# Another order of the SBUF pools in a fused attention and MLP kernel

## The chip, the cores and the metric

The kernel runs on one core of a Trainium2 chip. The metric is the device time of one execution in microseconds (us); the median of three runs of the kernel before is 382.42 us (380.60 to 382.48).

## What is computed

Three layers follow each other. The first is attention with a decaying state, over 2 batches, 8 heads, 768 positions and 64 elements per head. The second and third are gated feed-forward layers with a model width of 512 and an inner width of 1024. All data are float32.

```python
for t in range(S):                                    # attention, per head
    state = gamma * state + k[t] (outer) v[t]
    y[t] = scale * q[t] @ state
xk = mu_k * x + (1 - mu_k) * x_prev                   # second layer; x is y, heads joined
xr = mu_r * x + (1 - mu_r) * x_prev
v = relu(xk @ w_k) ** 2 @ w_v
x = sigmoid(xr @ w_r) * v
h = gelu(x @ w_in); u, v = halves of h                # third layer
v_n = (v - mean) / sqrt(var + 1e-6) * g_ln
out = x + (u * (w_sg @ v_n + b_sg)) @ w_out           # w_sg mixes the 768 positions
```

## The kernel before

The whole kernel is one straight list of operations. A planner (`Plan`) simulates the five engines with costs per operation and puts them in an order; each engine then runs its operations in exactly that order. The planner knows the tile pools by name, with a number of buffers for each.

The attention stage takes 12 chunks of 128 positions. For each, PE computes scores (sc, L407), the state (st, L443) and the output (y, L461 for the part from the state, L469 for the part within the chunk). These matmuls are plain float32, and a trace shows two PE instructions for each. sc uses two halves of 64 partitions side by side; the y matmul of L461 uses all 128 partitions.

Everything after it works on blocks of 512 columns (2 batches by 256 positions, 3 blocks). Each operand is split into a high part in fp32r and the rest, also in fp32r, and a product is made of three passes (high by high, high by low, low by high). `dense` (L310) issues all of these matmuls, so that they all have line L318. The groups are, in the trace's names: kp<-xo,wk (moving operand xo, stationary wk), rp<-xo,wr, vp<-k,wv, vp<-win,x2o (moving win, stationary x2o), up<-x2o,win, sp<-wsg,vh (moving wsg, 256 columns, the rest have 512) and op<-gt,wout. In the trace's names the moving operand doesn't always stand first; in the code it is `rhs`.

ACT and DVE convert the weights from the 8-byte words in which they are loaded (raw), into a tile cv and from there into the two fp32r tiles (hi by a cast at L237, lo by a subtraction at L289). They also clear out the PSUM results. After a kp tile ACT applies relu (L523), two squares (L528, L530), and DVE subtracts (L531). SP issues all DMAs.

Where each pool lies in SBUF follows from the order in which the pools are entered, one after the other from byte 16512 of each partition. The order is that of the dictionary `slots` (L196), and `cp`, with the constants, is the last.

```python
for name in slots:
    space = dict(space=bass.MemoryType.PSUM) if name == "ps" else {}
    pools[name] = ctx.enter_context(tc.tile_pool(name=f"{name}_p", bufs=slots[name], **space))
```

| pool | bytes per partition | start before | start mod 64 | what is in it |
|---|---|---|---|---|
| p4 | 17 x 4096 | 16512 | 0 | chunk, pr, xo, k (k2), x2o, vh, bsg |
| x | 3 x 8224 | 86144 | 0, 32, 0 | x and x2 |
| t | 8 x 2048 | 110816 | 32 | vs, cv, mix, rk, u, g, o |
| raw | 3 x 4096 | 127200 | 32 | weights as loaded, v of the third layer |
| small | 384 | 139488 | various | bn statistics and norm |
| aA, aB | 2 x 8192 each | 139872, 156256 | 32 | wk, then win, then gt |
| bA, bB | 2 x 9216 each | 172640, 191072 | 32 | scr (attention), wv, wsg |
| cA | 2 x 8192 | 209504 | 32 | wr, then wout |

The x pool's buffers are 8224 bytes, which is 32 more than a multiple of 64; three of them move what comes behind by 32. The PSUM pool ps has its own memory. Within a pool the buffers of p4, t, raw and of the weights are multiples of 64 bytes long, and the matmuls' columns in them begin at multiples of 512 bytes.

Of the kernel before, what the change touches and what calls it, by code (L numbers as in the profile page):

```python
# [28 lines left out]
NB = S // BW  # L29
# [163 lines left out]
def fused_kernel(ctx, tc, qk, kv, w_k, w_v, w_r, w_in, w_sg, w_out, consts, ydec, b_sg, out):  # L193
    nc = tc.nc
    pe, act, dve, pool, sp = nc.tensor, nc.scalar, nc.vector, nc.gpsimd, nc.sync
    slots = {"p4": 17, "x": NB, "t": 8, "raw": 3, "ps": 8, "small": 2, "aA": 1, "aB": 1, "bA": 1, "bB": 1, "cA": 1}  # L196
    plan = Plan(slots, {"p4": {"chunk": 6, "pr": 2, "xo": 4, "k2_0": 2, "k2": 8}, "ps": {"sc": 4, "y": 1},
                        "t": {"vs": 2, "cv": 2, "mix": 2, "rk": 2, "u": 6, "g": 2, "o": 2}},
                {("p4", "chunk"): 6, ("p4", "xo"): 8, ("t", "cv"): 4, ("ps", "sc"): 4})
# [584 lines left out]
```

## Time and profile before

| | us |
|---|---|
| median of 3 runs | 382.42 (380.60 to 382.48) |
| the profiled execution, its own time | 383.29 |
| its span, first to last instruction | 381.5 |
| PE busy | 370.1 |
| DVE busy | 248.6 |
| ACT busy | 159.0 |

Roughly, the attention stage runs until 54.8 us, the second layer until 226.5 us, the third layer's first product until 293.7 us, then sp and op in turn to 377.7 us. How to read it: the span holds one execution. PE is the matmul engine, DVE and ACT the two elementwise engines, POOL a third, and SP issues the DMAs. A busy PE is not PE at its peak, because matmuls are pipelined: the "mean ns of one" of a matmul covers its whole passage, and the distance from one start to the next is the shorter number that sets the time. The chain of work that ended last gives that distance, as the time of a piece divided by its count.

### The profile page before, as it was taken

The numbers are of one execution on the slowest core, as the hardware profiler recorded it, in microseconds if no ns is written. First come the engines' busy times: TensorE is split into PE (matmuls) and PEld (weight loads), VectorE is DVE, ScalarE is ACT, GpSimd is POOL, SyncE is SP. The second block draws the span as 40 slices with busy tenths as digits, with TensorE's granted clock in tenths as the row PEclk, the third lists the DMA queues.
The fourth block names the chain that finished last, engine by engine and source line by source line (L and its number), as shares of the span: only waits on it lengthen the run. The fifth ranks groups of instructions, "written<-read, shape, count | busy, mean of one in ns | idle before, by whom it ended". The sixth has DMA issues, their size and how long they took to land.

```text
span 381.5 us, 5546 instructions
## 1 busy us (share of the span) xinstructions
PE 370.1 (97%) x2218; PEld 308.8 (81%) x2218; DVE 248.6 (65%) x468; ACT 159.0 (42%) x266; POOL 20.1 (5%) x27
## 2 busy tenths in 40 slices
PE   6979999989999999999999999999999999999996
PEld 3978878868888888888888888888888999899884
DVE  2799999898898377312898637849385555516522
ACT  1357368998865575004889214414243000000000
POOL 2334510000000000000000000000000000000000
PEclk9889999989999999999999999999999999999999
DMA  7999455245530003300043101110111000020022
GB/s 263 415 363 411 190 168 165 70 145 159 180 111 0 0 3 110 110 2 0 9 158 110 42 2 41 27 54 3 41 44 41 2 0 2 27 84 0 29 110 82
DMA packets 11112, 35.97 MB, mean 94 GB/s; under 512 B 1232, under 2 KB 1360, under 8 KB 11088
## 3 DMA queue, kind: packets, MB, share of 16 engines
q1 hardware_dynamic: 11088, 35.63, 27.5%
q8 instruction: 17, 0.28, 0.3%
q14 instruction: 7, 0.06, 0.0%
HBM read 32.48 MB, written 3.15 MB: 93 GB/s over the span
## 4 chain that ended last, share of the span: by engine, by line
PE 90%; DMA 6%; DVE 1%; SPq 1%; ACT 1%; POOLq 0%; issue 0%
PE vp L318 26%; PE kp L318 18%; PE sp L318 13%; PE rp L318 9%; PE up L318 9%; PE op L318 9%; DMA chunk<-qk 3%; DMA scr<-ydec 2%; PE sc L407 2%; PE y L469 2%; DMA chunk<-kv 1%; PE y L461 1%; PE st L443 1%; DVE cv L285 0%; DVE cv L278 0%; DVE pr L416 0%
## 5 line engine op out<-in xcount | busy, mean ns | idle before, releaser
L318 PE MATMUL kp<-xo,wk 128*128 128x512 f32 x288 | 67.8, 395 | 0.0
L318 PE MATMUL vp<-k,wv 128*128 128x512 f32 x288 | 67.7, 395 | 0.0
L318 PEld LDWEIGHTS vp<-k,wv 128*128 128x128 f32 x288 | 54.0, 187 | 13.2
L318 PEld LDWEIGHTS kp<-xo,wk 128*128 128x128 f32 x288 | 53.9, 187 | 13.3 <-issue 0.2
L318 PEld LDWEIGHTS sp<-wsg,vh 128*128 128x128 f32 x432 | 51.4, 188 | 0.2
L318 PE MATMUL sp<-wsg,vh 128*128 128x256 f32 x432 | 51.4, 281 | 0.0
L318 PE MATMUL rp<-xo,wr 128*128 128x512 f32 x144 | 35.9, 409 | 1.8 <-ACT xo L237 1.8
L318 PEld LDWEIGHTS rp<-xo,wr 128*128 128x128 f32 x144 | 28.1, 195 | 9.2 <-ACT xo L237 2.3
L318 PE MATMUL vp<-win,x2o 128*128 128x512 f32 x144 | 34.1, 396 | 0.0
L318 PE MATMUL up<-x2o,win 128*128 128x512 f32 x144 | 34.1, 395 | 0.0
L318 PE MATMUL op<-gt,wout 128*128 128x512 f32 x144 | 33.1, 390 | 0.0
L318 PEld LDWEIGHTS vp<-win,x2o 128*128 128x128 f32 x144 | 27.1, 188 | 6.6
L318 PEld LDWEIGHTS up<-x2o,win 128*128 128x128 f32 x144 | 27.0, 187 | 6.6
L318 PEld LDWEIGHTS op<-gt,wout 128*128 128x128 f32 x144 | 26.9, 188 | 5.5
L531 DVE TENSOR_TENSOR k<-rk,k 128x512 fp32r<-128x512 f32 x24 | 16.6, 691 | 16.7 <-ACT rk L530 16.5
L528 ACT ACTIVATE k<-rk 128x512 fp32r<-128x512 f32 x24 | 15.2, 632 | 28.4 <-DVE rk L525 28.0
L543 DVE TENSOR_TENSOR x<-vp,x 128x512 f32<-128x512 f32 x12 | 8.3, 691 | 27.5 <-PE vp L318 27.5
L673 DVE SCALAR_TENSOR_TENSOR g<-sp,con,bsg 128x512 f32<-128x512 f32 x12 | 9.0, 752 | 26.0 <-PE sp L318 26.0
L285 DVE SCALAR_TENSOR_TENSOR cv<-raw,cv 128x512 int32<-128x512 int32 x32 | 24.5, 766 | 0.9
L263 ACT ACTIVATE cv<-raw 128x512 f32<-128x512 f32 x32 | 21.0, 667 | 3.3 <-DMA raw<-w_k 2.6
L689 DVE TENSOR_TENSOR o<-op,x 128x512 f32<-128x512 f32 x12 | 8.3, 692 | 20.4 <-PE op L318 20.3
L407 PE MATMUL sc<-chunk 64*128 64x128 f32 x192 | 15.7, 309 | 4.2 <-DMA chunk<-qk 4.2
(78 smaller groups left out, 425.2 us busy)
## 6 DMA issues: line engine op xcount, KB each, us to landing
chunk<-qk SPq DMA_DIRECT2D x12, 512.0 KB, 8.9
chunk<-kv SPq DMA_DIRECT2D x12, 512.0 KB, 8.5
raw<-w_k SPq DMA_DIRECT2D x8, 512.0 KB, 6.0
raw<-w_v SPq DMA_DIRECT2D x8, 512.0 KB, 3.7
raw<-w_in SPq DMA_DIRECT2D x8, 512.0 KB, 3.6
out<-o SPq DMA_DIRECT2D x12, 256.0 KB, 2.0
raw<-w_sg SPq DMA_DIRECT2D x6, 384.0 KB, 3.3
raw<-w_r SPq DMA_DIRECT2D x4, 512.0 KB, 4.5
```

Source lines behind the costliest of these rows:

```text
L263: plan.op("ACT", .68, lambda: act.activation(out=xf(), in_=word(1).bitcast(F32), func=ACTF.Copy, scale=F64_REBIAS), r=[(raw, 0)], w=[(xb, ...
L285: plan.op("DVE", .69, lambda: dve.scalar_tensor_tensor(out=xi(), in0=word(1), scalar=F64_SIGN, in1=xi(), op0=ALU.bitwise_and, op1=ALU.bitw ...
L318: pe.matmul(out=T[ps][:, cols], lhsT=l(), rhs=r(), start=first and q == 0 and i == 0, stop=q == 2 and i == len(grp) - 1, skip_group_check= ...
L407: pe.matmul(out=T["sc", i, p][:, j * CH:(j + 1) * CH], lhsT=a[par[p], 1, j], rhs=a[par[p], 0, j], start=j == 0, stop=j == KD - 1, skip_gro ...
L443: pe.matmul(out=st[par[p], b, j], lhsT=T["kv", i][:, 0, h], rhs=T["vs", i][:, h], start=c == 0 and b == 0 and j == 0, stop=b == B - 1 and ...
L461: pe.matmul(out=T[y][:, j * CH:(j + 1) * CH], lhsT=T["sbd", (c - 1) % 2][:, b, j], rhs=T["qk", i][:, 0, j], start=j == 0, stop=False, skip ...
L469: pe.matmul(out=T[y][par[p], j * CH:(j + 1) * CH], lhsT=T["vs", i][:, 2 * j + p], rhs=T["pr", i][:, p, j], start=c == 0 and j == 0, stop=j ...
L528: plan.op("ACT", .63, lambda: act.activation(out=T[o][:, 0], in_=T[rk], func=ACTF.Square), r=[(rk, 0)], w=[(o, ("hi", 0))], new=[new_p("k2 ...
L531: plan.op("DVE", .69, lambda: dve.tensor_tensor(out=T[o][:, 1], in0=T[rk], in1=T[o][:, 0], op=ALU.subtract), r=[(rk, 0), (o, ("hi", 0))], ...
L543: plan.op("DVE", .69, lambda: dve.tensor_tensor(out=T[x2][:, m], in0=T[ps], in1=T[x2][:, m], op=ALU.mult), r=[(ps, 0)], w=[(x2, m)])
L673: plan.op("DVE", .75, lambda: dve.scalar_tensor_tensor(out=seg(T[g]), in0=seg(T[ps]), scalar=T["vec"][:, 2, m:m + 1], in1=T["bsg"][:, cols ...
L689: plan.op("DVE", .69, lambda ps=ps, o=o, m=m: dve.tensor_tensor(out=T[o], in0=T[ps], in1=T["x2", n][:, m], op=ALU.add), r=[(ps, 0), (("x2" ...
```

## The change

The dictionary `slots` has the same entries with the same numbers, in another order: first the weight pools, then p4, raw, t, (ps,) and last x and small.

```diff
-    slots = {"p4": 17, "x": NB, "t": 8, "raw": 3, "ps": 8, "small": 2, "aA": 1, "aB": 1, "bA": 1, "bB": 1, "cA": 1}
+    slots = {"aA": 1, "aB": 1, "bA": 1, "bB": 1, "cA": 1, "p4": 17, "raw": 3, "t": 8, "ps": 8, "x": NB, "small": 2}
```

By the sizes above the pools then start at 16512 (aA), 32896 (aB), 49280 (bA), 67712 (bB), 86144 (cA), 102528 (p4), 172160 (raw), 184448 (t), all 0 mod 64; the three x buffers at 200832, 209056 and 217280, which are 0, 32 and 0 mod 64; small at 225504, and cp at 225888 as before.

## Rows read from the trace of the kernel before

**Rows 1.** The page: span, and busy time (share) and instructions by engine.
```profile
span 381.5 us, 5546 instructions
PE 370.1 (97%) x2218; PEld 308.8 (81%) x2218; DVE 248.6 (65%) x468; ACT 159.0 (42%) x266; POOL 20.1 (5%) x27
```

**Rows 2.** Waits of PE: who waited for whom: total us, times, longest.
```profile
PE sc L407 <- DMA chunk<-qk: 4.2, 2, 2.3
...
PE rp L318 <- ACT xo L237: 1.8, 1, 1.8
...
PE y L469 <- POOL vs L421: 0.4, 1, 0.4
```

**Rows 3.** The chain that ended last, in time: start us, us, what, count.
```profile
79.96 12.31 PE rp L318 x45
92.27 22.40 PE vp L318 x96
114.67 22.40 PE kp L318 x96
137.07 11.20 PE rp L318 x48
...
237.87 11.20 PE up L318 x48
249.07 11.20 PE vp L318 x48
...
293.87 34.08 PE sp L318 x288
327.95 10.94 PE op L318 x48
338.88 17.04 PE sp L318 x144
355.92 21.82 PE op L318 x96
```

**Rows 4.** The same chain, in the attention stage.
```profile
10.81 11.39 DMA chunk<-qk
...
32.96 1.09 PE sc L407 x16
34.05 1.09 PE y L461 x8
```

**Rows 5.** Busy time by stretch: window, length, engines (count), granted clock, DMA.
```profile
92.10:114.50 22.40, 22.40 (x97) 17.99 (x96) 20.15 (x32) 18.17 (x32) 0.00 (x0) 1.00 0.52 161
...
148.10:170.50 22.40, 22.40 (x97) 17.99 (x96) 7.14 (x12) 3.33 (x6) 0.00 (x0) 1.00 0.22 67
...
327.80:338.70 10.90, 10.90 (x50) 9.00 (x49) 4.64 (x7) 0.00 (x0) 0.00 (x0) 1.00 0.19 72
```

**Rows 6.** Timeline of ACT, 77 to 80 us: start, us, operation, [idle before].
```profile
77.47 0.60 ACT L523 ACTIVATE rk<-kp 128x512 f32<-128x512 f32 x1 [0.30 <-PE kp L318]
...
79.30 0.60 ACT L237 CAST xo<-mix 128x512 fp32r<-128x512 f32 x1
```

**Rows 7.** Timeline of PE, DVE and ACT in the first vp block.
```profile
92.11 8.09 PE L318 MATMUL vp<-k,wv 128*128 128x512 f32 x34
...
103.51 0.69 DVE L543 TENSOR_TENSOR x<-vp,x 128x512 f32<-128x512 f32 x1 [1.18 <-PE vp L318]
...
108.81 0.62 ACT L237 CAST wv<-cv 128x512 fp32r<-128x512 f32 x1 [1.34 <-DVE cv L285]
```

**Rows 8.** Groups by form, DVE and ACT: count, busy us, mean ns, idle before.
```profile
L530 ACT ACTIVATE rk<-rk 128x512 f32<-128x512 f32 x24 | 15.2, 633 | 0.8
L528 ACT ACTIVATE k<-rk 128x512 fp32r<-128x512 f32 x24 | 15.2, 632 | 28.4 <-DVE rk L525 28.0
...
L531 DVE TENSOR_TENSOR k<-rk,k 128x512 fp32r<-128x512 f32 x24 | 16.6, 691 | 16.7 <-ACT rk L530 16.5
...
L307 DVE TENSOR_TENSOR gt<-g,gt 128x512 fp32r<-128x512 f32 x12 | 8.3, 692 | 0.4
```

**Rows 9.** DMA issues: count, KB each, median us from issue to landing.
```profile
raw<-w_sg SPq DMA_DIRECT2D x6, 384.0 KB, 3.3
...
bsg<-b_sg SPq DMA_DIRECT2D x1, 384.0 KB, 2.9
```

## The prediction

> **What bounds the kernel now.** I read four views in this order: the busy shares, the waits of PE, the chain that ended last in order of time, and the busy time by stage. The first says PE is busy 370.1 of 381.5 us [rows 1]. The second says how little of the rest is waiting: 4.2 us for q/k chunks in the opening, one wait of 1.8 us for a cast on ACT and one of 0.4 us [rows 2]. From 79.96 us to the last matmul nobody keeps PE waiting; the chain there consists of PE alone [rows 3]. So the time after the opening is the number of matmuls times the spacing of their starts, and only a change of that spacing can move the end.
>
> The spacing is the thing to look at. A chain row divided by its count gives it: 22.40/96 = 233.3 ns for kp and vp, 11.20/48 = 233.3 ns for rp, up and vp<-win, all with 512 columns [rows 3]. The output stage op has the same 512 columns, the same type, the same 128 rows, and takes less: 10.94 us for 48 and 21.82 us for 96, so that the additional 48 took 10.88 us, 226.7 ns each, plus some 0.06 us on entry [rows 3]. sp has 256 columns: 34.08/288 and 17.04/144, both 118.3 ns [rows 3]. [...]
>
> Does what runs beside PE explain the difference? No. vp takes 22.40 us with DVE busy 20.15 and ACT 18.17 us beside it, and the same 22.40 us with DVE 7.14 and ACT 3.33 us; sp takes 118.3 ns in both of its blocks [rows 3, 5]. So the quiet of the op stage (ACT 0.00 us [rows 5]) isn't what makes it fast.
>
> What does set op apart is the layout. Every L318 matmul except op's reads one operand from p4 (starts at 0 mod 64) and one from a weight pool (32 mod 64); op reads gt and wout, both from weight pools, both at 32 mod 64. So the fast spacing goes with equal starts modulo 64, the slow one with unequal ones, whichever operand is the moving one: kp moves the 0 side, vp<-win the 32 side, both are at 233.3 ns.
>
> **The change part by part.** The order of the instructions, their waits and their queues stay: the planner's dictionaries are looked up by name, and the sizes and counts are the same. Only addresses move. By the sizes, the weight pools, p4, raw and t all come to 0 mod 64; the middle x buffer remains at 32, and the small tiles and columns inside x are not aligned, but PE reads none of these.
>
> Step 1, the 512-column matmuls with unequal starts: kp, vp<-k 3 x 96 each, rp, vp<-win, up 3 x 48 each, together 1008. All come to equal starts. I take op's steady spacing for them: 1008 x (233.3 - 226.7) = 6.7 us off the path. op itself stays (equal before and after).
>
> Step 2, sp, 432 matmuls of 256 columns, vh from p4 and wsg from bA/bB: unequal now, equal after. No row shows 256 columns with equal starts. One end is no gain, 118.3 ns as now; the other takes the whole 6.7 ns per matmul of step 1 off, 432 x 6.7 = 2.9 us. [...]
>
> Step 3, sc, y and st of the attention stage. sc has both operands in p4 (equal), y<-chunk,scr has one in p4 and one in bB (unequal). In each partition both move four times 128 columns and load four times 128 weights per chunk, and both take 1.09 us [rows 4]. Here equal starts bring nothing, so I take 0 for this stage; these are plain fp32 matmuls, which read their columns more slowly than L318's fp32r.
>
> Step 4, DVE and ACT. The squares on ACT take 633 ns from t to t (equal) and 632 ns from t to p4 (unequal), and DVE's subtraction of the same shape takes 691 ns with operands in t and p4 (k<-rk,k) and 692 ns with all of them at 32 mod 64 (gt<-g,gt) [rows 8]. Cost and gain 0. If they should change by a few ns, PE's lack of waits covers it.
>
> Step 5, DMA. A 384 KB load into p4 (bsg) lands in 2.9 us, the same size into raw (w_sg, 32 mod 64) in 3.3 us as a median [rows 9]. That may be the alignment or the company. Four w_k loads of 512 KB go into raw before the q/k chunk that lands after 11.39 us [rows 4]; at most 4 x 0.4 x 512/384 = 2.1 us, capped by the second half of PE's 4.2 us wait, about 2 us. I take 0 and keep 2 us for the fast end, because bsg is one load with the queue to itself.
>
> Where the gain might be given back. After the first kp block PE waits 1.82 us for the cast of xo at 79.3 us. That cast stands on ACT behind the three operations on the last kp tile, the first of which waited only 0.30 us for PE [rows 6]. The kp block gets 96 x 6.7 = 0.64 us shorter; if everything else on ACT keeps its time, only 0.30 of it arrives, and 0.34 us is lost. ACT's earlier work there waits on PE too, so part moves along: I charge 0.2 us, bounds 0 and 0.6. The next tight place is the last wv piece: its cast ends at 108.81 + 0.62 = 109.43 us, and the 77th matmul of the first vp block, its first reader, starts near 92.1 + 76 x 0.2333 = 109.8 us, 0.4 us later [rows 3, 7]. The cast descends from a run of DVE work that began at 103.51 us after DVE had waited 1.18 us for PE [rows 7]; it therefore moves with PE, and between the two points PE gains only 28 x 6.7 = 0.19 us, less than 0.4. No charge.
>
> The sum: 6.7 + 1.7 - 0.2 = 8.2 us. The profiled execution took 383.29 us, 381.5 in the span and 1.8 around it; it would have 373.3 in the span and 375.1 us. The median of the runs shown, 382.42, lies 0.87 under the profiled one; from it the forecast is 374.2 us. Own range: with sp and the DMA at their best 382.4 - (6.7 + 2.9 + 2) = 370.8, say 371.0; with sp at nothing and 0.6 lost 382.4 - 6.1 = 376.3, say 376.5.
>
> **The rivals.** *No effect.* Alignment by 64 does nothing and op is fast for another reason of its own. For it: step 3's equal 1.09 us. Against it: same shape, same clock, other spacing, and no other engine explains it. The time stays at 382.4 us.
> [...]
>
> *Halves of SBUF, not bits within 64.* In every slow group the p4 operand lies below 131072 and the weight operand above it; in op both lie above. If equal halves are what counts, then after the change the weights are all below and p4 runs from 102528 to 172160, so 7 of 17 buffers are on the fast side: 7/17 x (6.7 + 1.7) = 3.5 us, 379.0 us. For it: the trace can't separate it from the forecast. Against it: the same comparison of sc and y.
>
> *Slower: the absolute start counts.* Each operand that starts at 32 mod 64 saves 6.7 ns rather than equality doing so. Then (32, 32) is op's 226.7, one of two is 233.3 whichever it is, and (0, 0) would be 240.0 ns. It fits every L318 row as well as the forecast does. Price: 1008 x 6.7 = 6.7, sp 1.7 the other way, and op loses both, 144 x 13.3 = 1.9 us: 10.3 us, 392.7 us. It decides as soon as the kp spacing after is above 233.3 ns. Against it: sc, the one (0, 0) case, is no slower than y with (0, 32) [rows 4]; and it would make the better-aligned start the worse one, for which nothing in the trace speaks.
>
> **How the numbers follow.** Forecast 0.70, halves 0.06, no effect 0.14, slower 0.10. The predicted time is the forecast's 374.2 us. Its own range holds nearly all of its 0.70; with the halves that is some 0.75, so the range must reach over the case without effect: 371.0 to 383.0 us, which leaves out the slower case and the far ends. Faster by over 0.5% (1.9 us, about what a measurement of this kernel can tell from no change) has the forecast and the halves, 0.76; within 0.5% has 0.14; slower has 0.10.
>
> **What would show it.** In the chain after, kp, vp and up near 10.88 us per 48 and rp likewise (step 1), sp near 114.4 ns a piece, 32.9 us for 288 (step 2), sc and y at 1.09 us (step 3), DVE and ACT means as before (step 4), the same 4.2 us of chunk waits (step 5), PE's wait for xo near 2.0 us, and no wait on wv. I'm wrong if kp stays at 22.40 us per 96, if it takes two values by p4 buffer (halves), or if it goes up to 23 us (absolute start), op with it.

## The result and the profile after

The changed kernel takes 376.85 us (median of 4 runs, 376.12 to 377.52) against 382.38 us before (median of 4 as well): a ratio of 0.9866 with a 95% interval of 0.983 to 0.990. The forecast was 374.2 us, its range 371.0 to 383.0. The profiled execution of the changed kernel took 377.21 us, 6.08 less than that of the kernel before.

The page of the changed kernel, first line of the span and busy time by engine:

```profile
span 375.4 us, 5546 instructions
PE 363.8 (97%) x2218; PEld 309.4 (82%) x2218; DVE 247.8 (66%) x468; ACT 158.8 (42%) x266; POOL 20.2 (5%) x27
```

PE's busy time fell by 6.3 us, with the same 2218 matmul instructions, and the span by 6.1; the others stayed (compare [rows 1]). The waits of PE in the changed kernel:

```profile
PE sc L407 <- DMA chunk<-qk: 3.5, 3, 2.7
PE rp L318 <- ACT xo L237: 1.8, 1, 1.8
PE st L443 <- issue: 1.2, 1, 1.2
```

They are about those of [rows 2]: 0.7 us less for the chunks, 1.2 us more at one st matmul, nothing for vs. So PE does the same work in less time, and the chain of the changed kernel says where (start us, us, what, count):

```profile
36.55 1.09 PE y L461 x8
...
39.13 1.09 PE sc L407 x16
...
54.66 22.00 PE kp L318 x96
...
79.17 12.09 PE rp L318 x45
91.26 21.76 PE vp L318 x96
113.02 21.76 PE kp L318 x96
134.78 10.88 PE rp L318 x48
...
232.70 10.88 PE up L318 x48
243.58 10.88 PE vp L318 x48
...
287.10 34.55 PE sp L318 x288
321.65 10.91 PE op L318 x48
332.56 17.27 PE sp L318 x144
349.83 21.80 PE op L318 x96
```

Against [rows 3], every 512-column group went from 233.3 to 226.7 ns (21.76/96, 10.88/48), op stayed where it was, and sp became slower: 34.55/288 = 120.0 ns instead of 118.3. From the start of the first kp block to the start of sp the kernel before took 239.03 us (54.84 to 293.87) and the changed one 232.44 (54.66 to 287.10), 6.59 less; sp gave 0.47 + 0.23 = 0.70 us back; op gained 0.05 and the opening 0.18. That is 6.12 us, all of the span's 6.1.

The opening varies from execution to execution by more than these last terms: in a later profile of the same changed kernel (after_third) the first kp block began at 53.34 us rather than 54.66, with a granted clock of 0.97 on average before it, against 0.94. That accounts for the 1.29 us between these two profiled executions (377.21 and 375.92 us). The first rp block varies too: its 45 matmuls took 12.09 us in the changed kernel's profile, at a granted clock of 0.86, and 10.49 us in that of gap_256 below, at 1.00. The profiles of the kernel before and of the changed kernel both have the lower clock there, so that the comparison above stands. Other profiles differ in it, and the spacings from the second kp block on, which repeat to 0.01 us in three profiles of the changed kernel, are the better witness below.

### The profile page after: what moved, and what is told of

Same layout as the page of the kernel before. It is cut to its first block, busy times and chain, and to the rows that moved or that the text cites. A ratio compares the mean times of both kernels' runs of the same rounds, so it can differ in the third digit from the quotient of the medians.

```text
span 375.4 us, 5546 instructions
## 1 busy us (share of the span) xinstructions
PE 363.8 (97%) x2218; PEld 309.4 (82%) x2218; DVE 247.8 (66%) x468; ACT 158.8 (42%) x266; POOL 20.2 (5%) x27
## 4 chain that ended last, share of the span: by engine, by line
PE 93%; DMA 4%; ACT 1%; issue 0%; SPq 0%; DVE 0%
PE vp L318 26%; PE kp L318 17%; PE sp L318 14%; PE rp L318 9%; PE op L318 9%; PE up L318 9%; DMA chunk<-qk 4%; PE sc L407 3%; PE y L469 3%; PE y L461 2%; PE st L443 2%; DVE o L689 0%; ACT k L528 0%; ACT rk L530 0%; ACT rk L523 0%
## 5 line engine op out<-in xcount | busy, mean ns | idle before, releaser
L318 PE MATMUL kp<-xo,wk 128*128 128x512 f32 x288 | 65.9, 389 | 0.0
L318 PE MATMUL vp<-k,wv 128*128 128x512 f32 x288 | 65.8, 389 | 0.0
L318 PE MATMUL rp<-xo,wr 128*128 128x512 f32 x144 | 35.0, 403 | 1.8 <-ACT xo L237 1.8
L318 PE MATMUL vp<-win,x2o 128*128 128x512 f32 x144 | 33.1, 389 | 0.0
L318 PE MATMUL up<-x2o,win 128*128 128x512 f32 x144 | 33.1, 389 | 0.0
L285 DVE SCALAR_TENSOR_TENSOR cv<-raw,cv 128x512 int32<-128x512 int32 x32 | 23.5, 735 | 0.9
```

Source lines behind the costliest of these rows:

```text
L285: plan.op("DVE", .69, lambda: dve.scalar_tensor_tensor(out=xi(), in0=word(1), scalar=F64_SIGN, in1=xi(), op0=ALU.bitwise_and, op1=ALU.bitw ...
L318: pe.matmul(out=T[ps][:, cols], lhsT=l(), rhs=r(), start=first and q == 0 and i == 0, stop=q == 2 and i == len(grp) - 1, skip_group_check= ...
```

## The experiments

The theory of the prediction, called E: a matmul is fast if its two operands begin at the same place modulo 64. Its rival, M, is the description of the change: they must begin at multiples of 64. In the kernel before only op had equal starts, and they were both at 32 mod 64.

**all32: equal starts, none at a multiple of 64.** The order of the kernel before with x moved to the front:

```diff
-    slots = {"p4": 17, "x": NB, "t": 8, "raw": 3, ...
+    slots = {"x": NB, "p4": 17, "t": 8, "raw": 3, ...
```

> The pools of the kernel before in the order x, p4, t, raw, ps, small, weights: p4, t, raw and every weight pool then begin at 32 mod 64, and no matmul operand begins at a multiple of 64. If what counts is that the two operands of a matmul begin at the same place modulo 64 (theory E, equality), all 512-column groups take 226.7 ns, sp 120.0 ns, and the time is that of the changed kernel, some 376.5 to 377 us. If what counts is that operands begin at multiples of 64 (theory M, multiples), kp, rp, vp and up stay at 233.3 ns or rise to 240.0, and the time is 382 us or more.

Measured: 382.01 us, ratio 0.9996 (0.997 to 1.002). No gain. The chain of all32:

```profile
113.61 22.31 PE kp L318 x96
...
247.49 11.16 PE vp L318 x48
...
292.15 34.18 PE sp L318 x288
...
354.53 21.81 PE op L318 x96
```

kp and vp<-win are at 232.4 ns (22.31/96, 11.16/48: 232.5) with both operands at 32 mod 64, while op, also at 32 and 32, is at its usual 227.2. So E has fallen: equality modulo 64 isn't enough. M isn't refuted by this run, but it can't explain op.

**sp_apart: only sp's operands apart.** sp was slower after the change (120.0 ns against 118.3), and E's explanation was that it, unlike the others, prefers unequal starts. wsg begins 32 bytes later inside its tiles; all weight tiles are 64 bytes longer:

```diff
-            T[buf] = [pools[tag].tile(list(shape), F32R, tag=f"{tag}{i}", name=f"{name}{i}") for i in range(2)]
+            n, at = shape[1] * shape[2], OFF.get(name, 0) // 4
+            T[buf] = [pools[tag].tile([128, n + PAD], F32R, tag=f"{tag}{i}", name=f"{name}{i}")[:, at:at + n]
+                      .rearrange("p (a b) -> p a b", a=shape[1]) for i in range(2)]
```

> The changed kernel with wsg's tiles begun 32 bytes later inside their buffers, so that sp's two operands differ by 32 mod 64 and all other pairs stay equal. Theory E with an extra that depends on the columns: sp goes back from 120.0 to 118.3 ns, the two sp blocks from 34.55 and 17.27 us to 34.08 and 17.04, 0.7 us less than the changed kernel in all, and the 512-column groups stay at 226.7 ns. Theory that sp is slower after the change for its place in SBUF or its neighbours and not for its starts: sp stays at 120.0 ns, no gain.

Measured: 379.51 us, ratio 0.9955 (0.993 to 0.998), slower than the changed kernel. Its chain:

```profile
111.30 22.23 PE kp L322 x96
...
289.06 34.06 PE sp L322 x288
```

sp did go back, to 118.3 ns, though as a mean of four tiles at four distances (160, 224, 288 and 352 bytes modulo 512, moving less stationary). But kp went to 231.6 ns, though all its operands began at multiples of 64, as did those of every group but sp. What the edit had also done is to lengthen each tile by 64 bytes, so that the four tiles of aA and aB were shifted by 0, 64, 128 and 192 bytes against each other. Multiples of 64 are not enough either.

**after_again: the yardstick.** The changed kernel, unedited, on the same chip.

> The changed kernel once more, on the chip of the other runs of this call, as their yardstick: 376 to 377.5 us, 512-column groups at 226.7 ns, sp at 120.0 ns.

Measured: 375.24 us, ratio 0.9838 (0.980 to 0.987), with kp at 21.76 us for 96 and sp at 34.55 and 17.27 us, as in the first profile.

**offsets_a: other offsets, several at once.** The edit of sp_apart with 128 bytes of padding per tile and an offset for each weight.

> The changed kernel with the weight tiles begun later inside their buffers by: wk 64, wr 128, wv 16, win 48, wsg 32, wout 32 bytes. Theory E with 64-byte lines: kp and rp stay at 226.7 ns, vp<-k, vp<-win, up and op go to 233.3 ns, op although neither of its operands lies in p4; sp 118.3. Rival, lines of 128: kp too is slow, only rp is fast. Rival, only the 32-byte half counts: vp<-k (16) stays fast and win (48) is slow. Rival, 16-byte lines: all stay at 226.7 ns. By theory E the time is that of the changed kernel plus 288 x 6.7 + 2 x 144 x 6.7 + 144 x 6.7 ns = 4.8 us less 0.7 us.

Measured: 380.21 us in a single execution. Its chain:

```profile
112.93 22.35 PE kp L322 x96
...
146.37 21.76 PE vp L322 x96
...
190.49 11.09 PE rp L322 x48
...
352.28 22.36 PE op L322 x96
```

kp (64 bytes) is slow, 232.8 ns; vp<-k (16 bytes) is fast, 226.7; op (32 bytes, no operand in p4) is slow, 232.9, so that p4 as such has nothing to do with it. rp, offset by 128, is in between, 231.0 ns. None of the four expectations fits all of these. What I had overlooked is the distance over a longer range than 64 or 128 bytes: the padding of 128 bytes per tile moved the tiles against each other, so that rp's low-part tile (a third of the matmuls) lay 0 mod 512 from p4 and its high-part tile 128. In the trace, from start to start, the former took 228.1 ns on average and the latter 232.8.

That gave theory D: what counts is the distance of the two operands modulo a larger number, 256 or 512. The distances, moving less stationary, mod 512: before, kp 32 and vp<-win 480; all32, 128 and 384; the changed kernel, 0 and 0; op, which has both operands in weight pools, 0 in both kernels and in all32. Four runs put this to the test.

**gap_384: all operands at multiples of 64, at distances of 384 and 128.** The pool small (384 bytes) stands between cA and p4:

```diff
-    slots = {"aA": 1, "aB": 1, "bA": 1, "bB": 1, "cA": 1, "p4": 17, ..., "x": NB, "small": 2}
+    slots = {"aA": 1, "aB": 1, "bA": 1, "bB": 1, "cA": 1, "small": 2, "p4": 17, ..., "x": NB}
```

> The changed kernel with the pool small (384 bytes) moved from the end to the place between cA and p4. Every operand of a matmul still begins at a multiple of 64, even of 128, but p4 lies 384 mod 512 from the weight pools. New theory, D: what counts is the distance of the two operands modulo 512, and 0 is the fast one; then kp, rp, vp<-k and up have 384 and vp<-win 128, the distances that the run all32 had, at 232.4 ns: 22.31 us for 96 instead of 21.76; op stays at 226.7 ns; the time goes back to some 381 to 382 us. Theory M (multiples of 64 are fast): 226.7 ns and 375 to 377 us. In all32 both operands were at 32 mod 64, so M is not yet refuted by it; here it is.

Measured: 381.53 us, ratio 1.0009 (0.999 to 1.003). Its chain:

```profile
113.50 22.31 PE kp L318 x96
...
236.22 11.20 PE up L318 x48
...
292.20 34.56 PE sp L318 x288
...
354.96 21.81 PE op L318 x96
```

The whole gain is gone, with every matmul operand at a multiple of 64: kp 232.4 ns, up 233.3, op still 227.2. M has fallen. (sp, here at 128, stayed at 120.0 ns.)

**x_first: no operand at a multiple of 64, at a distance of 0.** The changed kernel with x at the front; the weight pools and p4 then begin at 32 mod 64.

> The changed kernel with the x pool moved to the front: every weight pool and p4 begin at 32 mod 64, none at a multiple of 64, and the distance of p4 to the weights stays 0 mod 512. Theory D: 226.7 ns in all 512-column groups, sp 120.0 ns, and the changed kernel's time, 375 to 377 us. Theory M: 233 ns or more and 381 us or more, as with all32.

Measured: 375.96 us, ratio 0.9846 (0.981 to 0.988). Its chain:

```profile
111.22 21.76 PE kp L318 x96
...
285.30 34.55 PE sp L318 x288
```

The whole gain is there without a single aligned operand. With gap_384 this settles it: alignment to 64 is neither needed (kp 226.7 ns here, at 32 and 32) nor enough (232.4 ns there, at 0 and 0).

**sp_apart_512: sp apart, all else at a distance of 0.** As sp_apart, but only wsg's tiles are padded, by 512 bytes, so that the others keep their distance.

```diff
+            n, at, pad = shape[1] * shape[2], 0, 0
+            if name == "wsg":
+                at, pad = 8, 128
+            T[buf] = [pools[tag].tile([128, n + pad], F32R, tag=f"{tag}{i}", name=f"{name}{i}")[:, at:at + n] ...
```

> As sp_apart (wsg begins 32 bytes later, the rest of the changed kernel), but wsg's tiles are padded to a multiple of 512, so that all other tiles keep their distance of 0 mod 512, which the 64 bytes of padding per tile in sp_apart had broken. Theory D: the 512-column groups are at 226.7 ns again, sp at some 117.8 to 118.3 ns, 0.7 to 1.0 us less than the changed kernel: 374.5 to 376 us. If sp_apart was slow for the shift of wsg itself, this one is slow too, 379 us.

Measured: 375.07 us, ratio 0.9814 (0.978 to 0.985). Its chain:

```profile
113.47 21.76 PE kp L322 x96
...
287.55 33.60 PE sp L322 x288
...
332.06 16.80 PE sp L322 x144
```

kp is fast again, and sp is at 116.7 ns, faster than before the change (118.3, at a distance of 480) and than after it (120.0, at 0).

**gap_256: a distance of 256.** gap_384 with small's tile bs lengthened, so that the pool has 768 bytes.

> As gap_384, with the pool small made 768 bytes long, so that p4 lies 256 mod 512 from the weight pools. If the period of theory D is 512: slow, 231 to 233 ns, 380 to 382 us. If it is 256: 226.7 ns, 375 to 377 us. sp_apart had this distance in one weight tile, for 12 or 16 matmuls at a time, at 228.3 ns on average, between the two.

Measured: 373.93 us in a single execution, with sp at 34.55 us for 288. From its chain:

```profile
77.45 10.49 PE rp L318 x45
...
109.74 21.76 PE kp L318 x96
```

256 is as good as 0, 226.7 ns in kp at both, so for 512 columns and distances that are multiples of 64 these runs show a period of 256, not 512. Of the others in it, 128 is slow (kp 232.4 ns in all32, the same in gap_384 at 384). So are 64 and 192: kp in offsets_a had these two alone, modulo 256, and its matmuls took 231.8 and 233.3 ns from start to start in the trace. That this time lies 3.28 us below the changed kernel's 377.21 isn't the distance: the opening was 1.72 us shorter, and the first rp block, at a granted clock of 1.00 rather than 0.86, took 1.60 us less.

**distances: small distances, with the period kept.** Each weight tile is 256 bytes longer and has its own offset.

> The changed kernel with every weight tile padded by 256 bytes, so that distances modulo 256 are kept, and begun later by: wk 16, wr 144, wv 8, win 240, wout 4, wsg 16 bytes. The distances of moving to stationary operand mod 256 are then kp 240, rp 112, vp<-k 248, up 16, vp<-win 240, op 252, sp 16. Theory D in its strict form (only 0 mod 256 is fast): all 512-column groups between 231 and 234 ns, op included. Theory D with a width (the distance must lie on one side of 0, within a line of 16 or 32 bytes, as 112 and 240 did in offsets_a at 226.7 to 227.7 ns): kp, rp, vp<-k, vp<-win and op at 226.7 ns, up at 233 ns. sp at 16: 120.0 ns if it belongs to 0, 116.7 ns if to 32, which sp_apart_512 had. If any 512-column group comes below 226.7 ns, a better place exists than the changed kernel's.

Measured: 380.92 us in a single execution. Its chain:

```profile
112.94 22.40 PE kp L322 x96
135.34 11.20 PE rp L322 x48
146.54 22.14 PE vp L322 x96
...
235.77 10.92 PE up L322 x48
246.69 11.20 PE vp L322 x48
...
290.91 34.17 PE sp L322 x288
...
353.05 22.32 PE op L322 x96
```

kp (240) and vp<-win (240) are at 233.3 ns, rp (112) too, vp<-k (248) at 230.6, op (252, that is 4 bytes off) at 232.5, and up (16) at 227.5. The strict form of D holds for the groups but up, with vp<-k a little under the 231 ns that it forecast; the form with a width on the side of 240 is refuted, and the width, if there is one, would be on the other side. This contradicts offsets_a, where vp<-k at 112 and 240 was at 226.7. The two runs differ in the padding between the tiles, 128 and 256 bytes. So for distances that aren't multiples of 64 the distance modulo 256 alone doesn't determine the spacing; what else does stays open. No 512-column group in any run was faster than 226.7 ns.

sp, at 16 modulo 256, fits neither of its two forecasts: its first block took 34.17/288 = 118.6 ns, its second 16.81/144 = 116.7, with the operands at the same distances. all32 has the like at 384 (118.7, then 17.29/144 = 120.1). And in sp_apart kp meets a distance of 0 for eight matmuls in a row, after four at 448: in the trace only the last two of the eight come at 225 to 227 ns each time, while the medians of the first six lie between 228 and 236 ns. So a matmul's spacing can depend on more than its own two addresses; that the matmuls before it play a part would fit, but no run here tests it.

**x_padded: the gain without the change.** The kernel before in its own order, with x's tiles 96 bytes longer, which puts the weights 256 mod 512 from p4:

```diff
+            if kind == "x":
+                n = KD * B * (BW + 1)
+                T[buf] = pools[pl].tile([128, n + 24], dt, tag=pl, name=str(kind))[:, 0:n].rearrange(
+                    "p (a b t) -> p a b t", a=KD, b=B)
+                return
```

> The kernel before, in its own order of the pools, with one edit: the tiles of the x pool are 96 bytes longer, so that the weight pools move by 288 bytes and lie 256 mod 512 from p4 (as in gap_256). Theory D: the whole gain without the change of order, kp, rp, vp, up at 226.7 ns, sp 120.0 ns, 375 to 377 us, ratio 0.983 to 0.988. If the place of the pools counts (weights low in SBUF, p4 higher), the time stays at 380 to 382 us.

Measured: 375.65 us, ratio 0.9872 (0.984 to 0.990). From its chain:

```profile
88.92 5.28 DMA raw<-w_v
...
109.95 21.76 PE kp L323 x96
...
284.04 34.55 PE sp L323 x288
```

So it isn't the place of the pools that counts here, but their distance: kp is at 226.7 ns with the pools in the old order. One thing more is to be seen here, in the waits of PE and the timeline of its first vp block:

```profile
PE vp L323 <- ACT wv L242: 0.3, 1, 0.3
...
105.12 1.20 PE L323 MATMUL vp<-k,wv 128*128 128x512 f32 x4 [0.29 <-ACT wv L242]
```

PE waits 0.29 us for the last wv piece, at the point that the prediction named as the next tight one; in the changed kernel's profile no such wait appears. The chain shows where it comes from: not from PE, as the prediction had it, but from a w_v load of 5.28 us, whose conversion ends in that cast.

**after_third and sp_apart_512_b: which is best.** The two kernels side by side on one chip.

> The changed kernel beside x_padded and sp_apart_512 on one chip: ratio to the kernel before 0.983 to 0.987, 512-column groups 226.7 ns, sp 34.55 and 17.27 us.

> sp_apart_512 once more, beside the changed kernel: sp at 116.7 ns, its blocks 33.60 and 16.80 us, 1.4 us less than the changed kernel's 34.55 and 17.27, everything else alike; so a ratio 0.003 to 0.004 below that of after_third. If the profile's 1.4 us is made up elsewhere, the two ratios are equal.

Measured: 376.09 us, ratio 0.9858 (0.983 to 0.989), and 374.27 us, ratio 0.9817 (0.980 to 0.984). The medians differ by 1.8 us; the profiles' sp blocks, 33.60 and 16.80 against 34.55 and 17.27 us, by 1.42. The ratios differ by 0.0041, about as expected, though their intervals touch. The chain of sp_apart_512_b:

```profile
78.38 10.49 PE rp L322 x45
...
284.78 33.60 PE sp L322 x288
```

In after_third the first rp block took 12.11 us, at a granted clock of 0.86 against 1.00 here, so the two profiled times (375.92 and 373.46 us) differ for that reason too, and the medians may. What is shown is sp's spacing, 1.42 us in all. By its spacings sp_apart_512 is the best of the kernels tried, some 1.8% below the kernel before.

## Why the prediction was right, and where its reason was wrong

The measured 376.85 us lie in the stated range, 371.0 to 383.0, but 0.35 us above the forecast's own range, which ended at 376.5. Step 2 brought the time to that end (382.4 less the span's 6.1 us are 376.3), and the medians, which move by as much between executions, past it. Of the signs that the prediction named, those on kp, vp, up, rp, sc, y and wv came; sp did not (34.55 us for 288 instead of 32.9), the chunk waits were 3.5 us instead of 4.2, and the wait on xo 1.8 instead of 2.0.

*Bound and place of the gain.* PE's spacing was the bound, and the gain lies in it and nowhere else: 6.59 us there, 6.12 in all after what sp gave back. Right.

*Step 1, 1008 matmuls by 6.7 ns.* Right in size: 226.7 ns in kp, rp, vp and up, 6.6 us. Wrong in its reason. The prediction read "equal modulo 64" out of [rows 3] because in the kernel before it couldn't be told from "a distance of 0 modulo 256": op was the only fast group, and had both. The order of the change happens to put p4 at a distance of 0 mod 512 from every weight pool, since all the pools between are multiples of 512 bytes long; that is what gives the gain. all32 and x_first show the difference. So the size came out right by luck: had the same equal starts come with a distance of 128, as in all32, the gain would have been nil. Reading the addresses modulo 64 only, because the change's description spoke of 64, was the mistake.

*Step 2, sp.* This is the term that was mis-sized, and it has the wrong sign: the forecast had sp at 114.4 ns, 1.7 us less than before, and it came at 120.0 ns, 0.7 us more. That is 2.4 us between them, a little more than the 2.1 us that are missing between the forecast gain of 8.2 us and the span's 6.1. No run shows the 1.7 us: it was an estimate of mine, between the step's two ends of 0 and 2.9 us, and what the runs showed in its place are the 0.7 us lost. The step assumed that 256 columns can only gain where 512 do. They didn't: at a distance of 0 the five slow 512-column groups came from 233.3 to 226.7 ns, and sp went from 118.3 to 120.0 ns. The one bound of the step, no gain, excluded a loss without a reason; it should have reached beyond zero, since nothing showed a 256-column matmul at such a distance.

*Steps 3 and 4.* Right. sc and y take 1.09 us before and after, and the squares and subtractions are as in [rows 8]; from the changed kernel's groups by form (count, busy, mean ns, idle before):

```profile
L530 ACT ACTIVATE rk<-rk 128x512 f32<-128x512 f32 x24 | 15.2, 633 | 0.8
...
L531 DVE TENSOR_TENSOR k<-rk,k 128x512 fp32r<-128x512 f32 x24 | 16.6, 691 | 15.5 <-ACT rk L530 15.2
```

*Step 5, DMA.* Right to take 0: loads into raw land in 3.2 us as a median with raw at 0 mod 64, 3.3 before [rows 9], and bsg's in the same 2.9:

```profile
raw<-w_sg SPq DMA_DIRECT2D x6, 384.0 KB, 3.2
...
bsg<-b_sg SPq DMA_DIRECT2D x1, 384.0 KB, 2.9
```

The w_k loads, which the 2 us at the fast end rested on, have a median of 4.4 us instead of 6.0, but it doesn't follow raw's start: 6.5 us in sp_apart_512_b, with raw at 0 mod 64, and 5.0 in all32, with raw at 32. Three of the four w_k loads were issued ahead of the q/k chunk, which SP issued at 10.81 us; the fourth, at 19.45 us, stood behind it, so that the step's bound of 2.1 us should have been 1.6.

*Given back.* The 0.2 us for the wait on xo weren't paid: the wait is 1.8 us as before, and ACT's first operation on the last kp tile, which had waited 0.30 us for PE [rows 6], still waited 0.23, so ACT moved along nearly whole. The wv piece held in the changed kernel; x_padded shows that its 0.4 us are not safe, and that a load (5.28 us there) and not PE can set that cast.

*The rivals.* "No effect" is out for this change by the time. But its premise, that alignment by 64 does nothing and op is fast for a reason of its own, is what gap_384 and x_first showed (kp at 232.4 ns with all operands aligned, at 226.7 with none); the order of the pools just happened to bring that reason, the distance, to the other groups. "Halves" is out: kp has one value, 226.7 ns, with p4's buffers on both sides of 131072. "The absolute start counts" is out by x_first, which is as fast at 32 and 32 as the changed kernel at 0 and 0 (kp 226.7 ns in both). PE's spacing isn't free of where its two operands lie: moving one against the other by 32 or 128 bytes moves it between 226.7 and 232.4 to 233.3 ns.

## What to carry to other kernels

Where PE is the bound and each matmul brings its own weights, divide a chain row by its count in each group; if groups of one shape differ, compare the byte addresses of moving and stationary operand, over several hundred bytes and not only modulo the alignment one has in mind. Here the fast distance for 512 columns was 0 modulo 256, where all matmuls of a group had it (226.7 against 233.3 ns), and 32 modulo 512 was the best of those tried for 256 columns (116.7 against 120.0 ns), so each of the two sizes had its own place. An experiment that pads tiles changes every distance behind it; keep the sums of sizes at multiples of 512 (256 was as good here, 226.7 ns in gap_256), or the edit measures something else, as sp_apart did, where kp went to 231.6 ns.

## What the runs showed of the hardware that was not expected

- The spacing of fp32r matmuls with a new weight tile each depends on the distance of the two operands in SBUF: 226.7 ns at 0 and 256, 232.4 to 233.3 ns at 32, 128, 384 and 480 (mod 512), for 512 columns. A shift of 4 bytes, beside multiples of 256, is enough to lose it in op (232.5 ns in distances).
- For 256 columns the order is another: 116.7 ns at 32, 118.3 at 480, 120.0 at 0, 256 and 128. At 384 and at 16 the two sp blocks of one run differ: 118.7 and 120.1 (all32), 118.6 and 116.7 (distances).
- At a distance of 0 and a granted clock of 1.00 a matmul of 512 columns took 226.7 ns and one of 256 columns 120.0 ns, so that the 256 columns more took 106.7 ns.
- The plain fp32 matmuls of the attention stage don't show it: 16 of sc, at a distance of 0, and 8 of y (L461), at 32 before and at 0 after, took 1.09 us in both kernels.
- In two executions of one kernel the 45 matmuls of the first rp block took 12.12 us (sp_apart_512) and 10.49 us (sp_apart_512_b), at granted clocks of 0.86 and 1.00.
- Left open: what decides at distances that aren't multiples of 64, where weights begun 16 bytes later were fast in vp<-k of offsets_a (226.7 ns) and slow in kp of distances (233.3 ns); why the first matmuls after a change of distance can be slow (medians of 228 to 236 ns in sp_apart); and the mechanism, which no run shows.
